# Attention and two MoE layers on one core: scores of batches 1 to 3 from float16 parts, with q and k turned by DMA

## The chip, the cores and the metric

The kernel runs on one core of one Trainium2 chip, in one launch. The metric is the device time of the launch in microseconds; lower is better. Three runs of the kernel before took 1101.78, 1102.73 and 1103.06 us, a median of 1102.73.

## What is computed

Attention with rotary position encoding (4 batches, 8 heads, 576 positions, 64 dimensions a head), then two MoE layers over 2304 tokens, all to float32 accuracy:

```
q_rot, k_rot = rotate(q), rotate(k)
scores = (q_rot @ k_rot.T) / sqrt(64)
scores = scores - max(scores, axis=-1)
attn = exp(scores); attn = attn / (sum(attn, axis=-1) + 1e-9)
x = attn @ v                                   # per batch and head, then tokens x 512
h = maximum(maximum(x @ w1, x @ w2), x @ w3)   # 512 -> 768
y = h @ w_out                                  # 768 -> 512
h2 = y @ w_in                                  # 512 -> 2048
out = (h2 * sigmoid(h2)) @ moe2_w_out          # 2048 -> 512
```

## The kernel before

**Attention.** Two heads form a pair; a batch has four pairs, so there are 16. A pair has five query tiles (four of 128 positions, one of 64), which makes 80 tiles in all. The order is: for each batch, tiles 0 and 1 of its four pairs, then tiles 2 to 4 of its four pairs; so all four pairs of a batch must be ready within the first eight of its twenty tiles. Numbered through, batch 1 begins with tile 20, batch 2 with tile 40, batch 3 with tile 60.

`attention()` issues one tile a step. `tile_scores` computes 128 rows of scores against 576 keys of both heads into the single PSUM buffer `s` (three banks): one matmul with the small block matrix `kd` for the 64 last keys of each head (L355), then three float32 matmuls that use 64 rows of the array each, the first for one head and the other two for the other (L358). `tile_max` takes the row maxima with their sign turned on VectorE (`nb`, L365), and two exponentials on ScalarE read `s` with that as their bias (L372). A step later `tile_norm` divides (L382 to L385), and two steps later `tile_turn` transposes the weights on TensorE (L401); `av` multiplies with v (L416, L420).

**Preparing a pair.** `load_qk` brings q and k of the pair into a `raw` tile (three buffers). `qk_rope` rotates them in place, for batch 0 on VectorE, later on GpSimd in nine instructions (L311 to L315). `qk_turn` turns them with nine float32 transposes on TensorE (L326, L332) and copies the result out of PSUM into `T` and `kd` with two instructions of ScalarE (L328, L333) and three of VectorE (L330, L336). `at(j, ...)` binds these calls to a step j: the rope six tiles before the pair's first tile, the turn three before.

**Beside it.** MoE 1 of a batch runs on TensorE between the tiles of the next one (`group`, L484, three float16 passes for each product of weights and values that are each split in two float16 parts); its results are evacuated by ScalarE and VectorE (L500 to L509). In the same time the weights of MoE 2 are read, narrowed on VectorE, GpSimd and ScalarE (L205, L206, L219, L220, L135) and written to scratch memory (`narrow_w2`). MoE 2 follows at the end (L484 and L728).

**What sets the order.** The program is issued step by step as above, and a list scheduler then orders each engine's instructions. On the chip each engine, and each engine's DMA queue, works its list strictly in that order. SyncE (SP) issues nearly all DMAs.

## Time and profile before

| | |
|---|---|
| median of the runs | 1102.73 us |
| the profiled execution | 1099.8 us, its span 1098.0 us |
| TensorE (PE) busy | 1019.9 us, 93% |
| VectorE (DVE) busy | 568.4 us, 52% |
| ScalarE (ACT) busy | 501.0 us, 46% |
| GpSimd (POOL) busy | 242.3 us, 22% |
| mean granted TensorE clock | 0.978 of full speed |

The span is the time from the first to the last instruction of the program. An engine's busy time counts its instructions but not its waits, register work or DMA issues. PEld is TensorE's loading of weights, which runs beside the matmuls. The matmuls overlap in the array, so the start of one to the start of the next says more than the length of one. A float32 matmul shows as two records in the trace (L355 x2 is one, L358 x6 are three). L484 is both MoE layers' helper, so its rows are told apart by time and shape.

### The profile page before, as it was taken

To read this page: it belongs to the slowest core of one execution; us is meant where nothing else is said; L and a number is where in the kernel's file an instruction comes from. 1 tells how busy PE (TensorE), PEld (TensorE's weight loads), DVE (VectorE), ACT (ScalarE), POOL (GpSimd) and SP (SyncE) were. 2 spreads that over 40 slices of the span, in tenths; PEclk is the share of its full clock that TensorE was granted. 3 is DMA by queue.
4 is the path that set the end of the run, shared out by engine and by line. 5 is a ranking of instruction groups with operands and counts; after the bars stand their busy time and mean duration, and the time that the engine had idled before them with its cause. 6 is when DMAs were issued, how large, how long until landed. Compare 5 with 4: busy or idle time off the path is not lost.

```text
span 1098.0 us, 16337 instructions
## 1 busy us (share of the span) xinstructions
PE 1019.9 (93%) x6250; PEld 625.9 (57%) x6250; DVE 568.4 (52%) x1108; ACT 501.0 (46%) x1200; POOL 242.3 (22%) x255
## 2 busy tenths in 40 slices
PE   2487899999998999999999988999999999999997
PEld 1344675766675776667766566644444444444554
DVE  5958667533577475475565568323434123423322
ACT  3668786645766667666677731122212012101111
POOL 1596117700136441051111126100000000000000
PEclk9789998999999999999999999999999999999999
DMA  7634022300334422132323173000101000100000
GB/s 195 192 109 125 13 91 57 98 1 7 98 94 126 125 87 94 44 90 91 88 87 91 63 284 120 13 13 10 49 10 48 20 20 1 39 20 1 20 20 20
DMA packets 79390, 76.10 MB, mean 69 GB/s; under 512 B 44752, under 2 KB 61648, under 8 KB 78288
## 3 DMA queue, kind: packets, MB, share of 16 engines
q1 hardware_dynamic: 75760, 65.03, 19.7%
q10 hardware_dynamic: 3552, 10.03, 2.7%
q8 instruction: 49, 0.80, 0.3%
q14 instruction: 29, 0.24, 0.1%
HBM read 57.21 MB, written 17.83 MB: 68 GB/s over the span
## 4 chain that ended last, share of the span: by engine, by line
PE 73%; DVE 5%; POOL 2%; DMA 1%; ACT 1%; issue 1%; DVEq 0%; SPq 0%; POOLq 0%
PE m L484 37%; PE o L728 17%; PE s L358 6%; PE tr L401 5%; PE xp L420 5%; PE s L355 1%; POOL wi L155 1%; PE xp L416 1%; PE tr L326 1%; DVE wi L158 1%; DVE nb L365 1%; DMA z<-in_moe_w_out_dram 1%; ACT e L372 1%; DVE vmax L145 1%; DVE wo L158 1%
## 5 line engine op out<-in xcount | busy, mean ns | idle before, releaser
L484 PE MATMUL m<-x,w 128*128 128x320 f16 (+1 forms) x1632 | 230.4, 289 | 7.5 <-ACT t L500 3.9
L728 PE MATMUL o<-wo,g 128*128 128x512 f16 x828 | 193.2, 379 | 0.0
L484 PEld LDWEIGHTS <-w 128*128 128x128 f16 x1632 | 157.1, 99 | 58.6 <-issue 18.3
L484 PE MATMUL m<-yt,wi 128*128 128x512 f16 (+1 forms) x920 | 189.8, 358 | 0.0
L714 ACT ACTIVATE gt<-m,ch 128x512 f32<-128x512 f32 (+1 forms) x80 | 51.5, 644 | 297.0 <-PE m L484 282.6
L365 DVE TENSOR_REDUCE nb<-s 128x2 f32<-128x1152 f32 (+1 forms) x80 | 108.3, 1353 | 81.8 <-PE s L358 81.5
L728 PEld LDWEIGHTS <-g 128*128 128x128 f16 x864 | 84.5, 98 | 99.7
L484 PEld LDWEIGHTS <-wi 128*128 128x128 f16 x920 | 89.6, 98 | 89.4
L372 ACT ACTIVATE e<-s,nb 128x576 f32<-128x576 f32 (+1 forms) x160 | 116.6, 734 | 48.7 <-DVE nb L365 40.1
L401 PE MATMUL tr<-ident,e 128*128 128x128 f32 (+1 forms) x720 | 113.1, 273 | 16.0 <-ACT pt L405 6.9
L385 ACT ACTIVATE e<-e,rec 128x576 f32<-128x576 f32 (+1 forms) x160 | 114.9, 766 | 15.8 <-DVE rec L383 15.7
L157 DVE TENSOR_SCALAR g<-gt,sg 128x512 f16<-128x512 f32 (+1 forms) x80 | 36.7, 458 | 162.8 <-ACT gt L714 162.8
L206 POOL TENSOR_SCALAR z<-z 128x256 uint16<-128x256 uint16 x64 | 53.6, 838 | 269.6 <-DVE z L205 255.6
L401 PEld LDWEIGHTS tr<-ident,e 128*128 128x128 f32 (+1 forms) x720 | 80.0, 142 | 41.9 <-ACT pt L405 10.8
L358 PE MATMUL s<-T 64*128 64x512 f32 (+5 forms) x480 | 103.0, 508 | 0.0
L405 ACT ACTIVATE pt<-tr 128x384 f32<-128x384 f32 (+1 forms) x160 | 70.2, 452 | 42.5 <-PE tr L401 41.7
L420 PE MATMUL xp<-pt,vd 128*64 128x256 f32 (+1 forms) x512 | 88.4, 422 | 0.0
L358 PEld LDWEIGHTS s<-T 64*128 64x128 f32 (+1 forms) x480 | 55.2, 185 | 37.4 <-issue 15.3
L484 PE MATMUL m<-h,wo 128*128 128x256 f16 (+1 forms) x512 | 73.9, 287 | 0.0
L502 DVE SCALAR_TENSOR_TENSOR t<-m,t 128x256 f32<-128x256 f32 (+1 forms) x96 | 43.4, 452 | 48.8 <-PE m L484 48.0
L420 PEld LDWEIGHTS xp<-pt,vd 128*64 128x64 f32 x512 | 38.0, 137 | 35.9 <-issue 17.3
L484 PEld LDWEIGHTS <-wo 128*128 128x128 f16 x512 | 49.2, 98 | 15.5 <-issue 3.1
(158 smaller groups left out, 1069.8 us busy)
## 6 DMA issues: line engine op xcount, KB each, us to landing
z<-in_moe_w_in_dram SPq DMA_DIRECT2D x32, 256.0 KB, 3.2
z<-in_moe_w_out_dram SPq DMA_DIRECT2D x32, 256.0 KB, 3.0
w<-in_moe_w_dram ACTq DMA_DIRECT2D x6, 768.0 KB, 6.7
wo<-in_moe_w_dram ACTq DMA_DIRECT2D x6, 768.0 KB, 4.8
qk<-in_q_dram SPq DMA_DIRECT2D x32, 128.0 KB, 3.0
qk<-in_k_dram SPq DMA_DIRECT2D x32, 128.0 KB, 3.0
vd<-in_v_dram SPq DMA_DIRECT2D x16, 256.0 KB, 2.9
zwi<-z SPq DMA_DIRECT2D x32, 128.0 KB, 2.9
```

Of the source, the lines that this page charges most:

```text
L206: nc.gpsimd.tensor_scalar(out=q[:, :, 2], in0=q[:, :, 1], scalar1=step, scalar2=off, op0=ALU.mult, op1=ALU.add)
L358: nc.tensor.matmul(s[0:n, o:o + m], qs[r], kt[r, a:a + m], start=True, stop=True)
L365: x = nc.vector.tensor_reduce(out=nb[0:n], in_=s[0:n, 0:1152].rearrange("p (h k) -> p h k", h=2), op=ALU.max, axis=AX.X, negate=True)
L372: x = nc.scalar.activation(out=e[0:n, HK[g]], in_=s[0:n, HK[g]], func=AF.Exp, bias=nb[0:n, g:g + 1], accum_out=sm[0:n, g:g + 1])
L385: nc.scalar.activation(out=e[0:n, HK[g]], in_=e[0:n, HK[g]], func=AF.Copy, scale=r[0:n, g:g + 1])
L401: nc.tensor.transpose(tr[:, i * n:(i + 1) * n], e[0:n, c * P:(c + 1) * P], ident[0:n, 0:n])
L405: nc.scalar.activation(out=to, in_=of, func=AF.Copy)
L420: nc.tensor.matmul(xp[r, 0:n], v4[:, g, c, :], pt[:, c + 5 * g, :], start=False, stop=(c == 3))
L484: nc.tensor.matmul(ps[:, 0:n], l, r, start=(i == 0), stop=(i == len(passes) - 1))
L502: nc.vector.scalar_tensor_tensor(out=t, in0=ps[:, 0:n], scalar=2.0 ** -22, in1=part[-1], op0=ALU.mult, op1=ALU.max)
L714: nc.scalar.activation(out=gt, in_=ps[:, 0:n], func=AF.Silu, scale=ch)
L728: nc.tensor.matmul(ps, l, r, start=(f == 0 and i == 0), stop=(f == NF2 - 1 and i == 2))
```

## The change

For batches 1 to 3 (12 of the 16 pairs, 60 of the 80 tiles), q and k are split after the rotation into two float16 parts each, high and low, with a power of two as scale for q and one for k. Batch 0 keeps the float32 way (`qk_turn32`, `tile_scores32`), with `kd` now a part of `T`.

- `qk_max`: three absolute maxima over the raw pair on VectorE, before the rotation. `qk_scale`: three transposes of one column and a small matmul on TensorE, a maximum and five tiny instructions on VectorE; the result is the two scales and the product of their inverses.
- `qk_turn`: ScalarE writes the high parts, six instructions (L366); VectorE subtracts them from the scaled values for the low parts, seven instructions (L367). High and low parts are stacked in `w` (now two buffers) so that one contraction over 128 rows sums high times high and low times high. The low parts of k stand in `fl`, a single tile. Three transposing DMAs on SP's queue (L387 to L389) turn 9, 9 and 6 blocks of 128 × 128 into `T`. Nothing of this uses TensorE or PSUM.
- `tile_scores`: eight float16 matmuls in place of four in float32; the last three multiply the high parts of q by the low parts of k, with 64 rows of the array each.
- `tile_max`: one more instruction on ScalarE (L474) multiplies the maxima by the inverse scale, and the exponentials take that as their scale.
- The steps: the load nine tiles before a pair's first tile, maxima eight before, rope and scale seven, turn five.

```diff
-    w_p = right("w_p", 1)
+    w_p = right("w_p", 2)
...
+    fl = [once.tile([P, 6, P], F16, name=f"fl{i}") for i in range(1)]
...
+    def qk_max(b, hp):
+        t = raw_t[b, hp]
+        m = small.tile([P, 3], F32, tag="qkm", name="qkm")
+        nc.vector.tensor_reduce(out=m[:, 1:2], in_=flat(t[:, 16:18, :]), op=ALU.max, axis=AX.X, apply_absolute_value=True)
+        x = [
+            nc.vector.tensor_reduce(
+                out=m[:, i:i + 1], in_=flat(t[:, lo:lo + 8, :]), op=ALU.max, axis=AX.X, apply_absolute_value=True
+            ) for i, lo in ((0, 0), (2, 8))
+        ]
...
+    def qk_scale(b, hp):
+        m = qkm_t.pop((b, hp))
+        ps = ps_m.tile([P, 512], F32, tag="m", name="m")
+        for i in range(3):
+            nc.tensor.transpose(ps[0:1, i * P:(i + 1) * P], m[:, i:i + 1], ident)
+        t = small.tile([1, 2], F32, tag="qkx", name="qkx")
+        nc.vector.tensor_reduce(out=t, in_=ps[0:1, 0:3 * P].rearrange("p (i x) -> p i x", i=2), op=ALU.max, axis=AX.X)
+        nc.tensor.matmul(ps[:, 384:386], ones, t, start=True, stop=True)
+        s, i = scale_of(ps[:, 384:386], 2, "qk", qks_p)
...
     def qk_turn(b, hp):
...
+        act(four(qh), head(0), s[:, 0:1])
...
+        for g in range(2):
+            act(
+                kh[:, g, 5:9, :].rearrange("p c (u d) -> p c u d", u=2),
+                t[:, 8 + g:16:2, :].unsqueeze(2).to_broadcast([P, 4, 2, D]), s[:, 1:2],
+            )
+        for g in range(2):
+            with tc.issue_after(last["max"]):
+                stt(four(ql)[:, g], head(0)[:, g], s[:, 0:1], four(qh)[:, g])
+            stt(L[:, 1:5, g * D:g * D + D], head(8)[:, g], s[:, 1:2], kh[:, g, 5:9, 0:D])
...
+        T = t_p.tile([P, 24, P], F16, tag="T", name="T")
+        nc.sync.dma_start_transpose(out=T[:, 0:9, :], in_=F[:, 0:9 * P])
+        nc.sync.dma_start_transpose(out=T[:, 9:18, :], in_=F[:, 9 * P:18 * P])
+        nc.sync.dma_start_transpose(out=T[:, 18:24, :], in_=L.rearrange("p c e -> p (c e)"))
...
     def tile_scores(key):
...
+        qa, qb = T[:, t * P:t * P + n], T[:, 1152 + t * P:1152 + t * P + n]
+        ka, kb, kl = T[:, 576:1152], T[:, 1728:2304], T[:, 2368:2944]
+        mm(0, qa, ka, 64, 512, **b0)
+        mm(512, qa, ka, 0, 64, **b0)
+        mm(512, qa, T, 3008, 64, **b1)
+        mm(576, qb, kb, 0, 448, **b0)
+        mm(1024, qb, kb, 448, 128, **b0)
+        mm(0, qa[lo], kl[lo], 64, 512, **b1)
+        mm(576, qb[hi], kl[hi], 0, 448, **b1)
+        mm(1024, qb[hi], kl[hi], 448, 128, **b1)
...
     def tile_max(key):
...
+            nc.scalar.activation(out=nb[0:n], in_=nb[0:n], func=AF.Copy, scale=inv)
...
-        at(u - 6 if i > 3 else i - 4, qk_rope, b, hp, nc.vector if i < 4 else None)
-        at(u - 3, qk_turn, b, hp)
+        if i > 3:
+            at(u - 8, qk_max, b, hp)
+            at(u - 7, qk_rope, b, hp)
+            at(u - 7, qk_scale, b, hp)
+            at(u - 5, qk_turn, b, hp)
+        else:
+            at(i - 4, qk_rope, b, hp, nc.vector)
+            at(u - 3, qk_turn32, b, hp)
```

The scheduler orders the changed program anew. Three places follow. The first is TensorE at the first tile of batch 2 (tile 40), in the kernel before: the four float32 matmuls of the scores, the transpose for the scale of v, and the transposes of a later pair (`qk`, `tr`).

```order
L484 LDWEIGHTS w_0_127
L484 MATMUL m_3336<-x_2020,w_0_127 128x256
L355 MATMUL s_3351<-kd_0_112,T_3049 128x128
L358 MATMUL s_3351<-T_3049 128x512
L358 MATMUL s_3351<-T_3049 128x384
L358 MATMUL s_3351<-T_3049 128x128
L112 MATMUL m_3394<-ident_78,vm_2_3392 1x128
L326 MATMUL tr_3297<-ident_78,qk_2509 128x128 x4
L332 MATMUL tr_3303<-ident_78,qk_2509 128x128
```

TensorE at a tile of batch 2 in the changed kernel (`T` holds the turned float16 parts, `tr` after it is the turn of the exponentials `e`):

```order
L449 MATMUL s_4316<-T_3785 128x512
L449 LDWEIGHTS T_3785
L449 MATMUL s_4316<-T_3785 128x64
L449 LDWEIGHTS T_3785
L449 MATMUL s_4316<-T_3785 128x64
L449 LDWEIGHTS T_3785
L449 MATMUL s_4316<-T_3785 128x448
L449 LDWEIGHTS T_3785
L449 MATMUL s_4316<-T_3785 128x128
L449 LDWEIGHTS T_3785
L449 MATMUL s_4316<-T_3785 128x512
L449 LDWEIGHTS T_3785
```

Four matmuls have become eight, each with its own weight load, and no transposes of `qk` stand on TensorE there any more.

The second place is VectorE between two row maxima (`nb`) shortly before batch 2, in the kernel before (`z` is the w2 narrowing, `t` and `h` are MoE 1's evacuation, `pt` the turned exponentials, `x` the attention's result):

```order
L365 TENSOR_REDUCE nb_2824<-s_2819 128x2
L219 TENSOR_SCALAR z_2781<-z_2781 128x256
L205 TENSOR_SCALAR z_2855<-z_2_2784 128x256
L407 COPY pt_2646<-tr_2845 128x3x64
L502 SCALAR_TENSOR_TENSOR t_2888<-m_2875,t_2873 128x256
L220 SCALAR_TENSOR_TENSOR z_2781<-z_1_2774,z_2781 128x256
L502 SCALAR_TENSOR_TENSOR t_2903<-m_2890,t_2888 128x256
L383 RECIPROCAL rec_2919<-rec_2919 128x2
L509 TENSOR_TENSOR h_5_2905<-t_2903,h_5_2905 128x256
L424 SCALAR_TENSOR_TENSOR x_2020<-xp_2940,vs_1696,x_2020 128x320
L365 TENSOR_REDUCE nb_2913<-s_2908 64x2
```

and behind a row maximum at that place in the changed kernel (`fl` and `w` with L367 are the subtractions for one pair, `qkx` the maximum for the scale of the next):

```order
L465 TENSOR_REDUCE nb_3250<-s_3241 128x2
L367 SCALAR_TENSOR_TENSOR w_3041<-qk_2844,qks_3059,w_3041 128x4x64 x2
L367 SCALAR_TENSOR_TENSOR fl_0_121<-qk_2844,qks_3059,w_3041 64x64 x2
L513 COPY pt_3153<-tr_3272 128x3x128
L221 TENSOR_SCALAR z_3206<-z_3206 128x256
L207 TENSOR_SCALAR z_3332<-z_2_3209 128x256
L367 SCALAR_TENSOR_TENSOR fl_0_121<-qk_2844,qks_3059,w_3041 128x4x64 x2
L222 SCALAR_TENSOR_TENSOR z_3206<-z_1_3199,z_3206 128x256
L621 TENSOR_TENSOR h_5_3129<-t_3127,h_5_3129 128x256
L614 SCALAR_TENSOR_TENSOR t_3239<-m_3226,t_3224 128x256
L326 TENSOR_REDUCE qkx_3308<-m_3304 1x2
```

Six subtractions and a maximum for the scale now stand among VectorE's other work between two row maxima.

The third place is SP's queue before batch 2 in the changed kernel (`z` loads and `zwi` stores are the w2 narrowing, `yscr` is MoE 1's result, `vd` is v):

```order
L768 DMA z_0_3082<-in_moe_w_in_dram 128x256
L749 DMA zwi_123<-z_2940 128x256
L639 DMA yscr_122<-y_2877 128x320
L387 DMA_TRANSPOSE T_3037<-w_2818 128x9x128
L388 DMA_TRANSPOSE T_3037<-w_2818 128x9x128
L389 DMA_TRANSPOSE T_3037<-fl_0_121 128x6x128
L288 DMA vd_0_120<-in_v_dram 64x64 x2
L768 DMA z_1_3199<-in_moe_w_in_dram 128x256
L749 DMA zwi_123<-z_2950 128x256
```

The three transposing DMAs of a pair stand between the narrowing's loads and stores; what follows them on SP is issued after them.

## Rows read from the trace of the kernel before

**Rows 1.** The page: the chain that ended last, by engine and by line.
```profile
PE 73%; DVE 5%; POOL 2%; DMA 1%; ACT 1%; issue 1%; DVEq 0%; SPq 0%; POOLq 0%
```
**Rows 2.** Stretches: start and end, length, busy per engine, clock, DMA share, GB/s.
```profile
40.00:60.00 20.00, 10.88 (x39) 7.14 (x39) 19.26 (x28) 13.69 (x30) 18.40 (x13) 0.65 0.43 127
...
141.50:199.90 58.40, 55.46 (x365) 37.50 (x363) 42.59 (x87) 40.89 (x102) 32.13 (x32) 0.94 0.32 87
199.90:298.30 98.40, 98.03 (x692) 67.64 (x692) 41.95 (x80) 59.34 (x148) 18.86 (x20) 1.00 0.12 36
298.30:343.80 45.50, 42.84 (x316) 30.74 (x315) 34.31 (x78) 30.45 (x84) 20.14 (x22) 1.00 0.43 118
...
452.10:496.90 44.80, 43.20 (x316) 30.69 (x314) 29.98 (x74) 28.99 (x78) 15.59 (x16) 1.00 0.27 78
496.90:630.40 133.50, 131.09 (x915) 89.80 (x912) 75.52 (x176) 93.89 (x254) 20.78 (x25) 0.99 0.27 81
...
318.60:336.70 18.10, 16.73 (x129) 11.91 (x130) 16.76 (x30) 11.15 (x32) 12.06 (x12) 1.00 0.49 132
```
**Rows 3.** The chain in order of time, 298 to 345 us: start, length, what.
```profile
319.86 2.99 DVE vmax L145 x4
...
326.79 3.12 DVE z L205 x3
...
333.51 4.22 DMA z<-in_moe_w_in_dram
```
**Rows 4.** TensorE's timeline: start, length, engine, line, operation, tiles, count.
```profile
249.55 3.42 PE L484 MATMUL m<-x,w 128*128 128x320 f16 x24
252.81 0.38 PE L355 MATMUL s<-kd,T 128*128 128x128 f32 x2
...
254.19 0.66 PE L401 MATMUL tr<-ident,e 128*128 128x128 f32 x4
```
**Rows 5.** The page: weight loads on L484, busy us and mean ns.
```profile
L484 PEld LDWEIGHTS <-w 128*128 128x128 f16 x1632 | 157.1, 99 | 58.6 <-issue 18.3
```
**Rows 6.** TensorE's timeline, transposes of q and k, what follows them.
```profile
335.49 0.66 PE L326 MATMUL tr<-ident,qk 128*128 128x128 f32 x4 [0.50 <-DVE pt L407]
...
336.09 1.47 PE L484 MATMUL m<-x,w 128*128 128x256 f16 x12
```
**Rows 7.** Groups by line and shape, 1 to 640 us: busy us, mean ns.
```profile
L330 DVE COPY T<-tr 128x512 f32<-128x512 f32 x16 | 11.0, 686 | 8.4 <-PE tr L326 8.4
L336 DVE COPY kd<-tr 64x64 f32<-64x64 f32 x32 | 7.0, 218 | 2.7 <-ACT T L333 2.4
L145 DVE TENSOR_REDUCE vmax<-vd 128x1 f32<-128x640 f32 x16 | 11.9, 809 | 0.0
L125 DVE TENSOR_SCALAR ve<-m 128x1 f32<-128x1 f32 x4 | 0.6, 146 | 0.0
L220 DVE SCALAR_TENSOR_TENSOR z<-z,z 128x256 int32<-128x256 int32 x64 | 30.8, 481 | 1.4
L328 ACT ACTIVATE T<-tr 128x512 f32<-128x512 f32 x16 | 9.4, 590 | 11.7 <-PE tr L326 11.7
L382 ACT ACTIVATE rec<-sm 128x2 f32<-128x2 f32 x64 | 13.2, 206 | 0.8 <-DMA qk<-in_k_dram 0.6
```
**Rows 8.** Line L355: what its engine waited for (us, times).
```profile
  ACT e L372: 18.7, 18
```
**Rows 9.** DMA issues: queue, operation, count, size each, median us to landing.
```profile
z<-in_moe_w_in_dram SPq DMA_DIRECT2D x32, 256.0 KB, 3.2
...
wo<-zwo SPq DMA_DIRECT2D x4, 1024.0 KB, 16.3
```
**Rows 10.** Timelines of DVE and of GpSimd: the same instruction at different times.
```profile
322.77 0.95 DVE L219 TENSOR_SCALAR z<-z 128x256 int32<-128x256 int32 x1
...
336.61 0.28 DVE L219 TENSOR_SCALAR z<-z 128x256 int32<-128x256 int32 x1
...
322.58 0.99 POOL L311 TENSOR_TENSOR w<-qk,sin_sb 128x384 f32<-128x384 f32 x1 [9.01 <-DMA qk<-in_q_dram]
```

More of the change, by code (lines that the diff above doesn't have):

```diff
@@ L99, in fused_kernel @@
     sin_sb = once.tile([P, 9, D], F32, name="sin_sb")
-    NK, NV = 4, 6
-    kd = [once.tile([P, P], F32, name=f"kd{i}") for i in range(NK)]
+    NV = 6
     vd = [once.tile([P, 5, P], F32, name=f"vd{i}") for i in range(NV)]
+    fl = [once.tile([P, 6, P], F16, name=f"fl{i}") for i in range(1)]
     yscr = dram.tile([P, KC, NT], F32, name="yscr")
@@ L258, in constants @@
         nc.gpsimd.affine_select(out=ident, in_=ident, pattern=[[-1, P]], compare_op=ALU.is_equal, fill=0.0, base=0, channel_multiplier=1)
-        for t in kd:
-            nc.gpsimd.memset(t, 0.0)
+        for t in fl:
+            nc.gpsimd.memset(t[:, 0:6:5, :], 0.0)
         for t in vd:
@@ L318, in qk_turn @@
     def qk_turn(b, hp):
+        t, W = raw_t.pop((b, hp)), w_t.pop((b, hp))
+        s, inv = sq_t[b, hp]
+        F = W.bitcast(F16)
+        L = fl[0]
+        qh = F[:, 0:38 * D].rearrange("p (g x) -> p g x", g=2)
+        ql = F[:, D:35 * D].rearrange("p (g x) -> p g x", g=2)
+        kh = F[:, 0:36 * D].rearrange("p (g c e) -> p g c e", g=2, e=P)
+        four = lambda x: x[:, :, 0:512].rearrange("p g (c e) -> p g c e", e=P)[:, :, :, 0:D]
+        head = lambda lo: t[:, lo:lo + 8, :].rearrange("p (c g) d -> p g c d", g=2)
@@ new lines, in qk_turn @@
+        rem = t[:, 16:18, :]
+        lo, hi = slice(0, 64), slice(64, 128)
+        act = lambda out, in_, sc: nc.scalar.activation(out=out, in_=in_, func=AF.Copy, scale=sc)
+        stt = lambda out, in0, sc, in1: nc.vector.scalar_tensor_tensor(
+            out=out, in0=in0, scalar=sc, in1=in1, op0=ALU.mult, op1=ALU.subtract
+        )
+        act(four(qh), head(0), s[:, 0:1])
+        act(qh[lo, :, 512:576], rem[lo], s[lo, 0:1])
+        act(qh[hi, :, 512:576], rem[hi], s[hi, 1:2])
+        act(ql[hi, :, 512:576], rem[hi], s[hi, 1:2])
@@ L320, in qk_turn @@
         t = raw_t.pop((b, hp))
-        T = t_p.tile([P, 576 + 512], F32, tag="T", name="T")
-        K = kd[(NP * b + hp) % NK]
+        w_t.pop((b, hp))
+        T = flat(t_p.tile([P, 24, P], F16, tag="T", name="T")).bitcast(F32)
+        K = T[:, 1088:1216]
+        nc.gpsimd.memset(K, 0.0)
         for i in range(2):
@@ L358, in tile_scores @@
             nc.tensor.matmul(s[0:n, o:o + m], qs[r], kt[r, a:a + m], start=True, stop=True)
+        return s
+    def tile_scores(key):
+        b, hp, t = key
+        T, inv = T_t[b, hp]
+        if inv is None:
+            s_t[key] = tile_scores32(t, T)
+            return
+        T = flat(T)
+        n = rows(t)
+        s = ps_s.tile([P, 1536], F32, tag="s", name="s")
+        lo, hi = slice(0, 64), slice(64, 128)
+        qa, qb = T[:, t * P:t * P + n], T[:, 1152 + t * P:1152 + t * P + n]
+        ka, kb, kl = T[:, 576:1152], T[:, 1728:2304], T[:, 2368:2944]
+        mm = lambda o, l, r, a, m, **kw: nc.tensor.matmul(s[0:n, o:o + m], l, r[:, a:a + m], **kw)
+        b0, b1 = dict(start=True, stop=False), dict(start=False, stop=True)
+        mm(0, qa, ka, 64, 512, **b0)
[6 more added lines that the diff above has]
+        mm(1024, qb[hi], kl[hi], 448, 128, **b1)
         s_t[key] = s
@@ L372, in tile_max @@
             x = nc.scalar.activation(
[L373 removed]
+                out=e[0:n, HK[g]], in_=s[0:n, HK[g]], func=AF.Exp, scale=inv, bias=nb[0:n, g:g + 1], accum_out=sm[0:n, g:g + 1]
             )
@@ L446, in fused_kernel @@
         if i > 2:
-            at(first[pairs[i - 1]] - (7 if hp == 3 else 9) if hp or i < 4 else first[b, hp] - 12, load_qk, b, hp)
+            at(first[pairs[i - 1]] - (7 if hp == 3 else 9) if i < 4 else u - 9, load_qk, b, hp)
         if i == 0:
             continue
-        at(u - 6 if i > 3 else i - 4, qk_rope, b, hp, nc.vector if i < 4 else None)
-        at(u - 3, qk_turn, b, hp)
+        if i > 3:
[3 more added lines that the diff above has]
+            at(u - 5, qk_turn, b, hp)
+        else:
+            at(i - 4, qk_rope, b, hp, nc.vector)
+            at(u - 3, qk_turn32, b, hp)
     for b in range(1, B):
@@ L805, in fused_kernel @@
     last["max"] = qk_rope(*pairs[0], nc.vector).ins
-    qk_turn(*pairs[0])
+    qk_turn32(*pairs[0])
     for j in sorted(e for e in events if e < 0):
```

31 lines of the change are left out of this document (23 added, 8 removed).

## The prediction

> **What bounds the kernel now.** I read the page's chain first: TensorE makes up 73% of the chain that ended last [rows 1]. MoE 2, after 740 us, runs on TensorE and isn't touched by the change; attention and MoE 1 share the time before. I cut that time at VectorE's (DVE's) row maxima, one for each of the 80 query tiles, so that the stretches in which q and k of a later batch are prepared stand alone: tiles 16 to 23, 36 to 41 and 56 to 61, which are 141.5 to 199.9, 298.3 to 343.8 and 452.1 to 496.9 us. Two of the stretches between them show TensorE busy 98 to 99.6% of the time, DVE 43 and 57% [rows 2]. In the three preparing ones TensorE drops to 94 to 96% and DVE rises to 67 to 75%. The chain inside the second one shows why: at 319.9 and again at 326.8 us it stays 3 us on DVE (four maxima of v; pieces of the w2 narrowing), and from 333.5 on 4.2 us on a load for that narrowing [rows 3]. In its worst 18.1 us DVE is busy 16.76; at the start, 40 to 60 us, 19.26 of 20 [rows 2]. So TensorE bounds most of attention, and DVE bounds the start and part of each preparation. The change takes work from the first and gives work to the second.
>
> **The change part by part, on the profiled execution's time** (1099.8 us: span 1098.0 and 1.8 around it; the median of the runs, 1102.73, is 2.9 more).
>
> *Scores, 60 of the 80 tiles.* In a dense stretch the old tile holds TensorE from 252.81 to 254.19 us, 1.38 us [rows 4]. The new one is eight float16 matmuls. Just before, 24 float16 matmuls of 320 columns take the 3.26 us from 249.55 to 252.81 [rows 4]: 136 ns each, 0.425 ns a column. So 512, 448, 128 and 64 columns take 218, 190, 54 and 27 ns, and each tile has two of every size. But a weight load is busy 99 ns [rows 5], so I let the four short ones take 100 ns each. All in a row that is 2×218 + 2×190 + 4×100 = 1.21 us. The last three use half the rows of the array each, one head in the upper and one in the lower half, like the old three on L358. If halves run side by side, one 218 goes: 1.0. With the short loads hidden too it is 0.8. I take 1.0, between the two: 0.38 × 60 = 23 us less (10 to 35).
>
> *The turn, 12 of 16 pairs.* TensorE loses nine transposes a pair. Five of them take the 0.60 us from 335.49 to 336.09 (the fifth is L332's) [rows 6]: 0.12 each, 1.1 a pair. It gains three of one column and a tiny matmul for the scale, which at 0.12 each are 0.5. Net 0.6 × 12 = 7 us less, so TensorE has 30 us less work in all.
>
> *DVE.* Per pair, removed: L330 0.69 and L336 twice 0.22, 1.1 us [rows 7]. Added: two maxima over 512 elements and one over 128 (L145 has 640 in 0.81; by share 0.65, 0.65, 0.2), 1.5; one over 384 on one partition, 0.5 by the same row; five tiny ones at 0.15 (L125), 0.75; four subtractions of 256 elements at 0.48 (L220), 1.9; three small ones at 0.22 (L336), 0.65. That is 5.3, net 4.2 us a pair and 50 us in all. In the dense stretches DVE has room for it. For the preparing stretches I priced what the new order puts between the same row maxima: about 20, 18 and 11 us of new work (the rest stands earlier or later), less 4.5 us removed in each: 15.5, 13.5 and 6.5. If DVE can be 94% busy (the mean of 16.76/18.10 and 19.26/20 [rows 2]), its room there is 54.9−42.6 = 12.3, 42.8−34.3 = 8.5 and 42.1−30.0 = 12.1 us. The first two overrun it by 3 and 5 us: 8 us longer. In those two TensorE's own saving (14 tiles × 0.38 and 8 pairs × 0.6, 10 us) then buys nothing. At the start the maxima of two pairs come between the second and fourth row maximum, where DVE is full: 3 us more.
>
> *ScalarE.* Per pair 2.4 us (three copies of 512 elements at 0.59 by L328, three small ones at 0.21 by L382) for the 0.8 removed (0.59 and 0.2). In each tile one more instruction, 0.21 us by L382 [rows 7], stands between the maximum and the exponentials, so the single score buffer comes free about 0.25 us later. L355 waited for the exponentials 18 times in 80 tiles [rows 8]; that is 14 times in 60, 3 us. Otherwise TensorE has MoE 1 work at hand, and ScalarE has room (59 of 98 us busy in the longer dense stretch [rows 2]). If that cover failed in every tile, it would be 15 us.
>
> *Transposing DMAs.* Three a pair on SP's queue (288, 288 and 192 KB), which wait there for DVE and ScalarE with the w2 loads behind them. No such DMA is in the trace. The nearest row is 256 KB landed in 3.2 us, the far one 1024 KB in 16.3 [rows 9]. So three take 10 to 49 us, one after the other; I take 11, near the closest size. The turn comes five tiles ahead (37 us, since 18 tiles take the 133.5 us from 496.9 on [rows 2]), so this is hidden, at nothing. The page "DMA: Bandwidth & Descriptors" of the Trainium skill, section "Latency and other measured facts", gives a transposing DMA 261 GB/s; by it the three would take an estimated 3 us, and no row here shows it.
>
> Sum: −30 + 8 + 10 + 3 + 3 = −6 us: 1093.8 in the profile, 1096.7 against the median shown.
>
> **The rivals.**
>
> *TensorE's saving arrives whole.* If the new work falls into DVE's gaps, the loss terms vanish: −30, 1073. For it: DVE idles 25 to 33% even of the preparing stretches [rows 2]. Against it: the chain through DVE at 320 us [rows 3].
>
> *Slower: DVE's subtractions swell beside GpSimd.* The same instruction on L219 took 0.28 us at 336.61 and 0.95 at 322.77; at the slow place GpSimd had just begun a rope, at 322.58 [rows 10]. GpSimd is busy 68 of the 148.7 us of the preparing stretches [rows 2], 46%, and a rope instruction takes 1.0 us. If each of the seven new subtractions of a pair is held for half of one, 46% of the time, that is 0.23 × 7 × 12 = 19 us of DVE, most of it where DVE then binds: about +15 on the forecast, 1112. From +6 us on the change is slower than the kernel before. The page "SBUF — State Buffer" of the Trainium skill, section "Who interferes with whom", speaks for it: a DVE instruction with two SBUF inputs contends with a GpSimd one that reads SBUF, and the later one blocks for the whole instruction. The new subtractions have two such inputs. But L220 has two as well, and its mean, such neighbours included, is 0.48 us [rows 7]; so this isn't the likeliest.
>
> *Slower: the transposes land late.* The tile that DVE writes for the third one (`fl`) is single, and the next pair's write to it comes two tiles, about 15 us, later. If the three take longer than that, DVE, which works its list in order, waits there with the row maxima behind it. At 20 us it is 5 us for each of nine pairs, 45, or 1142. In a mild form only the w2 loads behind them on SP are late, as one was already for 4.2 us [rows 3]: 12 × 1.5 = 18, 1115.
>
> *The scores don't get much shorter.* With 1.21 us a tile they give 10 instead of 23: 1110.
>
> **How the numbers follow.** Forecast 0.45 (its own range 1087 to 1104), whole saving 0.17, GpSimd 0.18, late transposes 0.12, scores 0.08. A measurement of this kernel can tell about 0.2% (2.2 us) from no change. Faster: the whole saving and three quarters of the forecast's weight, 0.51, and a little from mild forms of the others: 0.52. Same: a fifth of the forecast's and some of the slower cases': 0.13. Slower: 0.35. The time is the forecast's, 1096.7. The range from 1077 takes in the upper part of the whole saving, to 1117 the cases of GpSimd, of the scores and of mildly late transposes.
>
> **What would show it.** Right: score tiles of about 1.0 us on TensorE; DVE 44 to 54 us busier; TensorE's idle time grown in the preparing stretches and at 40 to 60 us; MoE 2 as before. For the whole saving: preparing stretches no longer than before. For GpSimd: subtractions of 256 elements above 0.6 us in the mean. For late transposes: landings above 5 us a piece, and DVE or TensorE waiting for them. I am wrong in kind if the dense stretches don't get shorter by some 0.3 us a tile.

## The result and the profile after

The changed kernel takes 1107.69 us (median of 7 runs, 1105.25 to 1111.21); the kernel before, run beside it, 1101.43 (1098.04 to 1103.06, 7 runs). The ratio is 1.0052 (95% interval 1.0039 to 1.0066): 0.5% slower, where 1096.7 and faster was forecast. The profiled execution's span (first to last instruction) is 1106.1 us, 8.1 longer than before.

Cut at the same row maxima, the two spans (and those of five experiments told below) divide like this, in us. "Preparing" is tiles 16 to 23, 36 to 41 and 56 to 61 together, "dense" the stretches between and behind them. Orders A and B are the changed kernel's work with its instructions in two other orders.

| stretch | before | after | order A | order B | DVE part alone | subtractions twice | scales of one, z moved |
|---|---|---|---|---|---|---|---|
| tiles 0 to 15 | 141.5 | 138.3 | 139.0 | 140.4 | 152.1 | 138.1 | 144.4 |
| preparing, 20 tiles | 148.7 | 178.1 | 166.0 | 169.0 | 165.1 | 176.2 | 143.8 |
| dense, 44 tiles | 340.2 | 320.9 | 324.6 | 319.3 | 358.5 | 331.1 | 327.7 |
| behind tile 79 | 467.6 | 468.8 | 468.9 | 476.0 | 467.9 | 475.1 | 467.0 |
| span | 1098.0 | 1106.1 | 1098.5 | 1104.7 | 1143.6 | 1120.5 | 1082.9 |

So TensorE's saving came, 19 us of it in the dense stretches, and the preparing stretches took 29 back. All three of them grew, by 7.5, 16.2 and 5.7 us. The windows of the changed kernel (length, then busy time and instructions of PE, PEld, DVE, ACT and POOL, granted clock, DMA share, GB/s), which answer to [rows 2]:

```profile
138.30:204.20 65.90, 54.59 (x357) 34.67 (x357) 55.86 (x133) 51.06 (x123) 35.26 (x33) 0.91 0.58 124
204.20:300.00 95.80, 92.36 (x669) 60.30 (x666) 44.49 (x86) 63.85 (x155) 16.37 (x18) 0.97 0.13 40
300.00:361.70 61.70, 48.40 (x354) 33.08 (x353) 56.44 (x127) 43.61 (x114) 34.83 (x36) 0.92 0.58 138
361.70:466.70 105.00, 102.55 (x758) 67.48 (x760) 66.91 (x163) 83.24 (x218) 24.20 (x27) 1.00 0.35 100
466.70:517.20 50.50, 42.52 (x318) 28.84 (x315) 40.57 (x96) 37.15 (x95) 23.75 (x25) 0.90 0.56 117
517.20:637.30 120.10, 116.10 (x857) 76.18 (x855) 73.04 (x169) 97.80 (x264) 20.60 (x25) 0.97 0.32 95
```

The first, third and fifth row are the preparing stretches. In them DVE is busy 80 to 91% of the time (67 to 75% before) and TensorE idles 32.6 us in all (7.2 before). TensorE's clock is 0.90 to 0.92 of 2.4 GHz there, 0.94 to 1.00 before. Of TensorE's waits in them 25.1 us end with DVE, against 5.6 before (11.3 of 20.9 us in order A, 20.9 of 25.5 in order B). The largest (who waited for whom: us in total, times, longest; the first two rows from the first stretch, then two from the second and one from the third):

```profile
PE m L327 <- DVE qkx L326: 3.1, 2, 2.3
PE tr L507 <- DVE pt L513: 3.0, 4, 1.9
PE m L596 <- DVE t L614: 4.7, 2, 3.4
PE m L117 <- DVE amax L116: 4.0, 1, 4.0
PE m L114 <- DVE t L614: 3.3, 1, 3.3
```

L327 makes the scale of q and k, L114 and L117 that of v; L614 evacuates MoE 1. Over the whole profile DVE is busy 616.6 us instead of 568.4 and ScalarE 550.9 instead of 501.0. The chain that ended last has less TensorE and twice the DVE of [rows 1]:

```profile
PE 67%; DVE 10%; POOL 3%; issue 3%; ACT 2%; DMA 2%; SPq 1%; DVEq 0%; POOLq 0%; ACTq 0%
```

A score tile on TensorE's timeline (start, length, engine, line, operation, tiles, count), against the 1.38 us of [rows 4]: seven matmuls hold it from 250.82 to 251.76, and the eighth, behind a piece of MoE 1, for 0.16 us. Over all 60 tiles L449 is busy 68.0 us by the page, 1.13 a tile.

```profile
250.82 1.00 PE L449 MATMUL s<-T 128*128 128x512 f16 x7
251.76 1.80 PE L596 MATMUL m<-x,w 128*128 128x320 f16 x12
253.49 0.23 PE L449 MATMUL s<-T 64*128 64x128 f16 x1
253.65 0.66 PE L507 MATMUL tr<-ident,e 128*128 128x128 f32 x4
```

DVE's new instructions and ScalarE's, by line and shape over 1 to 640 us (count, busy us, mean ns):

```profile
L367 DVE SCALAR_TENSOR_TENSOR fl<-qk,qks,w 128x256 f16<-128x256 f32 x24 | 12.9, 567 | 1.7 <-ACT w L366 1.5
L367 DVE SCALAR_TENSOR_TENSOR w<-qk,qks,w 128x256 f16<-128x256 f32 x24 | 12.0, 540 | 0.0
L367 DVE SCALAR_TENSOR_TENSOR fl<-qk,qks,w 64x64 f16<-64x64 f32 x24 | 7.7, 364 | 0.4
L311 DVE TENSOR_REDUCE qkm<-qk 128x1 f32<-128x512 f32 x24 | 16.0, 675 | 5.8 <-DMA qk<-in_q_dram 5.4 <-DMA qk<-in_k_dram 0.4
L128 DVE TENSOR_SCALAR qke<-qke 128x2 int32<-128x2 int32 x12 | 3.9, 324 | 0.1
L127 DVE TENSOR_SCALAR qke<-m 128x2 f32<-128x2 f32 x12 | 1.7, 145 | 1.7 <-PE m L327 1.5
L474 ACT ACTIVATE nb<-nb,qkv 128x2 f32<-128x2 f32 x48 | 14.0, 293 | 21.4 <-DVE nb L465 21.1
L478 ACT ACTIVATE e<-s,nb,qkv 128x576 f32<-128x576 f32 x96 | 78.9, 826 | 1.5 <-PE tr L507 0.3
L478 ACT ACTIVATE e<-s,nb 128x576 f32<-128x576 f32 x32 | 23.3, 736 | 6.2 <-DVE nb L465 6.2
```

The subtractions take 0.54 to 0.57 us where 0.48 was put down, the small ones 0.36 (one of three 0.48) for 0.22. And DVE's timeline inside the second preparing stretch, at a place where it has hardly a gap:

```profile
326.60 0.49 DVE L128 TENSOR_SCALAR qke<-qke 128x2 int32<-128x2 int32 x1
327.12 0.92 DVE L129 TENSOR_SCALAR qks<-qke 128x2 int32<-128x2 int32 x1
327.96 0.15 DVE L130 TENSOR_SCALAR qki<-qke 128x2 int32<-128x2 int32 x1
328.03 1.23 DVE L621 TENSOR_TENSOR h<-t,h 128x256 f16<-128x256 f32 x1
329.18 0.95 DVE L330 TENSOR_TENSOR qkv<-qki 128x1 f32<-128x1 f32 x1
330.06 1.34 DVE L465 TENSOR_REDUCE nb<-s 128x2 f32<-128x1152 f32 x1
331.32 2.98 DVE L147 TENSOR_REDUCE vmax<-vd 128x1 f32<-128x640 f32 x4
```

Operations on one or two values a partition last 0.15 or 0.9 us. GpSimd's rope instructions, which lie beside them:

```profile
325.11 2.92 POOL L343 TENSOR_TENSOR w<-qk,sin_sb 128x384 f32<-128x384 f32 x3 [2.09 <-DVE rec L489]
327.97 3.11 POOL L344 TENSOR_TENSOR qk<-qk,cos_sb 128x384 f32<-128x384 f32 x3
```

The turning DMAs land as early as taken (queue, operation, count, median us to landing), 3.3 + 3.3 + 2.8 for the 11 put down:

```profile
T<-w SPq DMA_TRANSPOSE x24, 3.3
...
T<-fl SPq DMA_TRANSPOSE x12, 2.8
```

### The profile page after: what moved, and what is told of

Read it like the earlier page. It is cut to its first block, busy times and chain, and to the rows that moved or that the text cites. A ratio compares the mean times of both kernels' runs of the same rounds, so it can differ in the third digit from the quotient of the medians.

```text
span 1106.1 us, 16556 instructions
## 1 busy us (share of the span) xinstructions
PE 999.0 (90%) x6202; PEld 595.9 (54%) x6202; DVE 616.6 (56%) x1264; ACT 550.9 (50%) x1308; POOL 239.3 (22%) x256
## 4 chain that ended last, share of the span: by engine, by line
PE 67%; DVE 10%; POOL 3%; issue 3%; ACT 2%; DMA 2%; SPq 1%; DVEq 0%; POOLq 0%; ACTq 0%
PE m L596 35%; PE o L840 17%; PE xp L526 5%; PE tr L507 4%; PE s L449 4%; DVE nb L465 2%; PE xp L522 1%; POOL wi L157 1%; DVE w L367 1%; DVE wi L160 1%; DVE z L221 1%; DVE fl L367 1%; POOL wo L157 1%; DVE pt L513 1%; DMA qk<-in_q_dram 1%
## 5 line engine op out<-in xcount | busy, mean ns | idle before, releaser
L596 PE MATMUL m<-x,w 128*128 128x320 f16 (+1 forms) x1632 | 231.5, 291 | 14.8 <-DVE t L614 7.6
L596 PEld LDWEIGHTS <-w 128*128 128x128 f16 x1632 | 158.3, 99 | 70.1 <-issue 30.2
L596 PE MATMUL m<-yt,wi 128*128 128x512 f16 (+1 forms) x920 | 189.8, 358 | 0.0
L596 PEld LDWEIGHTS <-wi 128*128 128x128 f16 x920 | 89.6, 98 | 89.4
L507 PE MATMUL tr<-ident,e 128*128 128x128 f32 (+1 forms) x720 | 115.9, 282 | 18.7 <-ACT pt L511 8.0
L478 ACT ACTIVATE e<-s,nb,qkv 128x576 f32<-128x576 f32 (+1 forms) x120 | 98.5, 825 | 1.7 <-PE tr L507 0.3
L511 ACT ACTIVATE pt<-tr 128x384 f32<-128x384 f32 (+1 forms) x160 | 69.6, 453 | 21.9 <-PE tr L507 21.5
L596 PE MATMUL m<-h,wo 128*128 128x256 f16 (+1 forms) x512 | 71.9, 288 | 1.5 <-DVE wo L160 1.3
L449 PE MATMUL s<-T 128*128 128x512 f16 (+1 forms) x480 | 68.0, 303 | 2.1 <-ACT e L478 1.9
L614 DVE SCALAR_TENSOR_TENSOR t<-m,t 128x256 f32<-128x256 f32 (+1 forms) x96 | 43.4, 452 | 43.4 <-PE m L596 35.4
L596 PEld LDWEIGHTS <-wo 128*128 128x128 f16 x512 | 49.0, 98 | 17.9 <-issue 3.2
L160 DVE SCALAR_TENSOR_TENSOR g<-gt,sg,g 128x512 f16<-128x512 f32 (+1 forms) x80 | 55.7, 696 | 2.5
```

The costliest lines, as they stand in the source:

```text
L160: nc.vector.scalar_tensor_tensor(out=l, in0=x, scalar=s, in1=h, op0=ALU.mult, op1=ALU.subtract)
L449: mm = lambda o, l, r, a, m, **kw: nc.tensor.matmul(s[0:n, o:o + m], l, r[:, a:a + m], **kw)
L478: x = nc.scalar.activation(out=e[0:n, HK[g]], in_=s[0:n, HK[g]], func=AF.Exp, scale=inv, bias=nb[0:n, g:g + 1], accum_out=sm[0:n, g:g + 1])
L507: nc.tensor.transpose(tr[:, i * n:(i + 1) * n], e[0:n, c * P:(c + 1) * P], ident[0:n, 0:n])
L511: nc.scalar.activation(out=to, in_=of, func=AF.Copy)
L596: nc.tensor.matmul(ps[:, 0:n], l, r, start=(i == 0), stop=(i == len(passes) - 1))
```

## Experiments

Each is compared with runs of the kernel before on the same chip; the changed kernel itself stands at 1.0052. Ratios below 1 are faster than the kernel before.

**DVE's work.** Theory A: DVE, full in the preparing stretches, sets their length. First, the change's DVE part alone, in the kernel before:

```diff
+            at(u - 8, more_max, b, hp)      # maxima over 512, 512 and 128
+            at(u - 7, more_scale, b, hp)    # one over 384 on one partition, five tiny
         at(u - 6 if i > 3 else i - 4, qk_rope, ...)
+            at(u - 4, more_sub, b, hp)      # four subtractions of 256, three of 64
```

> The change's DVE part alone: the kernel before with DVE instructions of the same kinds and sizes that the change adds for each of 12 pairs (two maxima over 512 elements and one over 128 eight tiles ahead, one over 384 on one partition and five tiny ones seven ahead, four subtractions of 256 elements and three of 64 four ahead), their results used by nobody. Scores, turning and ScalarE stay as they were. It is 5.3 us a pair, some 60 us of DVE, 40 of them in the preparing stretches, where TensorE was idle for 7 us. Theory A (DVE's extra work, where it is full, is the loss): 12 to 25 us slower, 1113 to 1126, with TensorE idle 15 to 30 us more there. Theory G (the loop through GpSimd's rope, ScalarE, DVE and the turning DMA): DVE's instructions fill its gaps, 1100 to 1108.

1143.36 us, ratio 1.038 (1.0345 to 1.0415): 42 us slower, more than expected. DVE's busy time rose by 80 us, not 60, to 648.7. Only 16 us of the loss lie in the preparing stretches; the start takes 11 and the dense stretches 18, which got shorter in the changed kernel. TensorE's busy time at 1.2 GHz, 35.1 us before, is 75.2. The preparing windows:

```profile
152.10:220.70 68.60, 58.82 (x357) 39.49 (x355) 57.47 (x122) 40.79 (x101) 30.13 (x28) 0.85 0.23 63
325.50:375.90 50.40, 44.59 (x310) 31.26 (x309) 44.00 (x97) 31.34 (x84) 22.19 (x22) 0.93 0.36 100
494.80:540.90 46.10, 40.91 (x291) 28.92 (x289) 38.06 (x87) 28.46 (x76) 16.62 (x16) 0.96 0.24 69
```

DVE is at 83 to 87% in them and TensorE idle 20.8 us: much of the picture of the changed kernel, without its scores. Second, the subtractions twice:

```diff
-        for g in range(2):
+        for g in (0, 1, 0, 1):
             ... stt(...)        # and the three small ones twice
```

> The changed kernel with each of the seven subtractions of a pair done twice, with the same result: 33 us more of DVE in the preparing stretches and a little outside, nothing else. Theory A: each us of DVE there costs 0.5 to 0.9, 1124 to 1137. Theory G: the turning DMA of a pair starts some 3 us later and the rope after it with it, but the turn is five tiles ahead: 1109 to 1118.

1123.38, ratio 1.0206 (1.0172 to 1.0239): 15.7 us over the changed kernel for 40 us more DVE (656.5). That is 0.6 us under theory A's range and above G's. But it didn't fall where A put it. The preparing stretches:

```profile
138.10:210.20 72.10, 55.38 (x368) 35.21 (x365) 70.23 (x159) 50.94 (x123) 39.29 (x35) 0.93 0.48 111
296.80:347.00 50.20, 41.66 (x306) 28.05 (x305) 47.93 (x110) 39.22 (x101) 25.93 (x27) 0.93 0.57 141
465.70:519.60 53.90, 40.66 (x294) 27.81 (x290) 49.77 (x113) 35.76 (x91) 25.00 (x25) 0.84 0.49 106
```

They are no longer than in the changed kernel (176.2 against 178.1; 7 to 10 longer than in orders A and B), although DVE works 15 us more in them: it is 92 to 97% busy, 95% in the mean. The loss lies in the dense stretches (10 us) and behind tile 79 (6). Third, without them:

```diff
-            stt(four(ql)[:, g], ...)   # and the other six; wz, fl zeroed once
+    wz = [once.tile([P, 19 * D], F32, name=f"wz{i}") for i in range(1)]   # stacked parts, in place of w
```

> The changed kernel without its seven DVE subtractions per pair: the low parts of q and k are zeros, written once. ScalarE's high parts, the maxima, the scales, the turning by DMA and all matmuls stay. In the changed kernel's three preparing stretches (138.3 to 204.2, 300.0 to 361.7 and 466.7 to 517.2 us, 178.1 us in all) the subtractions hold DVE for 12.2, 11.6 and 8.9 us, 32.7 in all. Theory A (DVE, full in these stretches, sets their length, and most of it is plain extra work): the stretches get 20 to 30 us shorter together and the kernel takes 1080 to 1089 us. Rival C (ScalarE's scaling holds the score buffer): the stretches keep their length within 5 us, 1103 to 1108. Rival D (the transposing DMAs make the loads behind them late): the same, 1103 to 1108.

1098.17, 0.9978 (0.9962 to 0.9995): 9.5 us gained, under a third of the DVE time: 9 us short of A's range, and outside those of C and D. Only its time is read here. It had to give the parts a tile of their own, which by itself costs (below, e7): against that run it gains 17.

**GpSimd's rope.** Rival B: DVE's instructions swell beside it. The rope of batches 1 to 3 was left out of both kernels:

```diff
-        for lo, hi in ((0, 18),) if eng else ((0, 6), (6, 12), (12, 18)):
+        for lo, hi in ((0, 18),) if eng else ():
```

> The changed kernel without the rotation (rope) that GpSimd applies to q and k of batches 1 to 3; GpSimd's other work stays. In the changed kernel, DVE's instructions in the three preparing stretches take about 30 us more than their own shortest tenth (8.1, 14.2 and 7.6), in the kernel before 15.6. Rival B (DVE's small instructions swell beside GpSimd's rope, and that is what lengthened the stretches): nearly all of these 30 us go, 1078 to 1085. Theory A (mainly plain extra work): a part of them goes, since GpSimd's rope is busy only half of the time, 1092 to 1100. Rivals C and D: 1103 to 1108.

> The control to the run before: the kernel before without the rotation of batches 1 to 3 on GpSimd. Theory A: its preparing stretches were only partly bound by DVE, so it gains little, 1093 to 1099, and the changed kernel without rope stays level with it (within 6 us either way). Rival B: it gains 5 to 10 us less than the changed kernel does by the same edit, so that the changed kernel without rope is at least 10 us faster than this one.

1085.03 (0.985, 0.9824 to 0.9875) and 1090.14 (0.9901, 0.9874 to 0.9929). The changed kernel gains 22.7 us and the one before 10.3; DVE's busy time falls by 30.7 (to 585.9) and by 18.5. The first is at the edge of B's range, but the two kernels without rope are 5 us apart, as A expected, and not 10. So the rope swells DVE's work by 12 us more in the changed kernel than in the one before. The 12 us more of time needn't all be swelling: without the rope its own time too is gone from the way of each pair, and orders spread (below). In the preparing stretches alone DVE's busy time falls from 152.9 to 127.8 us and, in the kernel before, from 107.0 to 97.6. The tiny operations show the swelling, without rope:

```profile
L128 DVE TENSOR_SCALAR qke<-qke 128x2 int32<-128x2 int32 x12 | 1.9, 157 | 0.1
L127 DVE TENSOR_SCALAR qke<-m 128x2 f32<-128x2 f32 x12 | 1.8, 147 | 2.8 <-PE m L327 2.7
```

L128 falls from 324 to 157 ns; L127, which reads PSUM, stays. The four tiny lines on SBUF together fall by 5.7 us, all subtractions by 4.0; the rest is older work, the narrowing of w2 above all.

**ScalarE's step between maximum and exponentials** (rival C). Doubled, left out (with the pointer in the exponentials), and alone in the kernel before:

```diff
+            nc.scalar.activation(out=nb2[0:n], in_=nb[0:n], func=AF.Copy, scale=inv)  # e12
-            nc.scalar.activation(out=nb[0:n], in_=nb[0:n], func=AF.Copy, scale=inv)   # e13
+            nc.scalar.activation(out=nb[0:n], in_=nb[0:n], func=AF.Copy, scale=inv)   # e14, inv = c1[0:n]
```

> The changed kernel with ScalarE's scaling of the row maxima done twice in 60 tiles (the first into a tile that nobody reads): 0.295 us more between the maximum and the exponentials of each, 18 us of ScalarE. Rival C (ScalarE's step there holds the single score buffer): 10 to 18 us slower, 1118 to 1126. Theories A and G: TensorE has other work at hand, 1107 to 1113.

> The changed kernel without ScalarE's scaling of the row maxima and without the scale pointer of the exponentials: the parts are made with a constant scale of one. The maxima and scales of q and k are still computed, and used by nobody, so DVE's and TensorE's work is the same. ScalarE loses 0.295 us a tile and 2 times 0.09 us at the exponentials, 28 us in all. Theory C (this step, in series between maximum and exponentials, holds the score buffer): as much gained as its doubling lost, 20 to 35 us, 1073 to 1088. Theory A (DVE's extra work is the loss): 1100 to 1107.

> The change's part on ScalarE between maximum and exponentials alone: the kernel before with the row maxima of batches 1 to 3 scaled by a constant one on ScalarE, and the same pointer as the scale of the exponentials. Nothing is left out. Theory C: 15 to 30 us slower, 1116 to 1131. Theory A: ScalarE has room in the kernel before, 1101 to 1107.

1138.64 (1.0345, 1.032 to 1.037), 1113.41 (1.0097, 1.0077 to 1.0118) and 1104.65 (1.0038, 1.002 to 1.0056). Doubling cost 31 us, leaving it out gained nothing and lost 6, adding it alone cost 2.8. The last two speak against C: each is far outside what it expected (e13 misses A's range too, by 6 us). Why a second 0.29 us a tile cost 31 isn't settled: 18 us of it lies in the dense stretches, where TensorE idled 9 us more and waited 5.3 us for the exponentials in the last one.

**Maxima and scales of q and k, and the step, all left out:**

```diff
-            at(u - 8, qk_max, b, hp)
-            at(u - 7, qk_scale, b, hp)
+        nc.gpsimd.memset(cs, 1.0)      # the constant scale
```

> The changed kernel with constant scales of one: the maxima of q and k, the scale that is made from them (three transposes, a matmul and seven DVE instructions a pair), ScalarE's scaling of the row maxima and the scale pointer of the exponentials are left out; the high and low parts, the turning and the matmuls stay. The maxima of q and k are about 2.75 us of DVE a pair, 33 us in all; ScalarE loses 0.295 us a tile and 2 times 0.09 us at the exponentials, 28 us in all. Theory A: the preparing stretches get 15 to 22 us shorter, the dense ones within 3 us as before, 1085 to 1093. Rival C (ScalarE): the dense stretches too get shorter, by 0.1 to 0.3 us a tile, and the whole falls to 1075 to 1083. Rival B: 1098 to 1104, since the rope still swells what is left.

1102.72 (1.0015, 0.9998 to 1.0033): 5 us gained, 10 short of A's range. The preparing stretches shrank by 21.9 us as A expected, but the start, the dense stretches and the end grew by 17.5. DVE's busy time fell by only 13.5 us of 33, partly since the subtractions swelled more (those into w from 540 to 737 ns).

**The loop through w, and late transposes** (theories G and D).

```diff
+    hl = once.tile([P, 19 * D], F32, name="hl")                    # e7: w_t[b, hp] = hl
-        nc.sync.dma_start_transpose(out=T[:, 0:9, :], ...)         # e11: all three twice
+        for _ in range(2): nc.sync.dma_start_transpose(...)
```

> The changed kernel with the stacked high and low parts in a tile of their own (hl, one buffer), and the rope's scratch w back to one buffer that only GpSimd uses. In the changed kernel GpSimd waited 8 times, 58.5 us in all, for the turning DMA to read w before it could start the next rope. Nothing is left out. Theory G: without that wait ropes come earlier, ScalarE and DVE no longer stand at a late pair's instructions, 1094 to 1102. Theory A: DVE's work is the same, 1104 to 1109. Theory F: no change by itself, 1104 to 1109.

> The changed kernel with each of a pair's three turning DMAs issued twice into the same tile: w is held 3 to 7 us longer, SP's queue holds 4 us more a pair, and the DMA engines move twice the bytes of it. Theory G (the loop through w's two buffers paces the pairs) and rival D (loads behind the turning DMAs are late): 10 to 30 us slower, 1118 to 1138. Theory A: within 4 us of the changed kernel, 1104 to 1112.

1115.10 (1.0126, 1.0094 to 1.0159) and 1119.78 (1.016, 1.013 to 1.019). GpSimd's 58.5 us of waiting for the turning DMA were gone in e7, and the kernel was 7 us slower: the ropes came earlier, into the start, which took 11.7 us longer, while the preparing stretches got 11.3 shorter. G's own prediction failed. Double turning cost 12 us: the lower end of what G and D expected, and outside A's range. Each DMA landed as early as before (3.4 and 2.8 us), and the preparing stretches got 3 us longer, the dense ones 5. So D in its mild form isn't refuted: in the changed kernel SP stood 46.5 us in all waiting for the subtractions in front of L387, with the loads behind it.

**TensorE's clock** (theory F).

```diff
+            for _ in range(5):
+                nc.tensor.matmul(s[:, 1152:1536], W1.h(1)[:, 0:P], W1.h(1)[:, 0:384], start=True, stop=True)
```

> The changed kernel with five extra float16 matmuls of 384 columns behind the scores of each of the 20 tiles 16 to 23, 36 to 41 and 56 to 61, into columns of the score buffer that nobody reads: 0.8 us a tile, 16 us of TensorE at full clock, in stretches where it was idle for 32.6 us. TensorE's records at half clock held 35.1 us of its busy time in the kernel before and 67.7 in the changed one. Theory F (the half clock after idle time is a large part of the loss): less busy time at half clock, 1098 to 1104. Theories A and G: the extra work falls partly into idle time and partly adds to the tiles, 1108 to 1122.

1106.56 (1.0049, 1.0029 to 1.0068): 16 us more of TensorE's work cost nothing. TensorE idled 97.5 us instead of 107.1, and 51.0 us of its busy time lay at 1.2 GHz instead of 67.7. The preparing stretches, which hold the added work, got 3 us longer. So TensorE's own work bounds them little. F's gain didn't come. Whether the extra work raised the clock isn't shown: other edits of the changed kernel, without such work, have 44 to 77 us at 1.2 GHz.

**The w2 narrowing (z) out of the preparing stretches**, in the changed kernel, the kernel before, and with scales of one:

```diff
-            for _ in range(1 + j % 2 if j > 31 else 0):
+            for _ in range(2 if j >= 24 and not (36 <= j <= 42 or 56 <= j <= 62) else 0):
```

> The changed kernel with the narrowing of the w2 weights (z) moved out of the three preparing stretches: its steps start at tile 24 instead of 31, two a tile, none at tiles 36 to 42 and 56 to 62. Nothing is left out. In the changed kernel's preparing stretches the narrowing holds DVE for about 1.9 us and GpSimd for 0.83 us a step, and 9 steps fall into the second and third stretch each. Theory A (DVE is full there, and relief of it shortens them): the second and third stretch lose 10 to 17 us each, the dense stretches, where DVE has room, at most 5 of it, 1085 to 1095. Theory G (the runs with one piece of DVE work taken away gave back less than a third of it, so the loop rope on GpSimd, high parts on ScalarE, low parts on DVE, turning DMA, and back to the rope's buffer paces the pairs): the narrowing isn't in that loop, 1100 to 1106. Theory F (a lower granted clock after TensorE's idle time is what costs): idle time goes with the narrowing, 1092 to 1100.

> The control: the same move of the w2 narrowing in the kernel before. Its preparing stretches have 7 us of TensorE idle time in all, so all theories expect little: 1094 to 1102. If the move gains as much here as in the changed kernel, its gain there says nothing about the change.

> Constant scales of one (as in the fourth run) and the w2 narrowing moved out of the preparing stretches (as in the fifth), together. Left out: the maxima and scales of q and k. DVE loses some 13 us in sum and 20 more in the preparing stretches. Theory A: with DVE no longer full there, 1085 to 1094. If something else fills the time that is freed, as in the fifth run, 1098 to 1104.

> As the run before it, and the MoE 1 work that is handed out per tile is 10000 columns in the preparing tiles and 7200 in the others, instead of 8000 everywhere (68 tiles: 5% less in attention, the rest after it). Theory A: TensorE's idle time in the preparing stretches (24 us with scales of one) is filled with work that the dense stretches lose, 1080 to 1092. If DVE or ScalarE is the limit there even so, the preparing stretches get longer by the added work, 8 to 15 us, and the dense ones shorter by as much: within 4 us of the run before it.

1106.98 (1.0063, 1.0041 to 1.0084), 1096.43 (0.9962, 0.9944 to 0.9981), 1085.04 (0.9846, 0.9825 to 0.9867) and 1089.53 (0.9883, 0.9864 to 0.9902). Alone the move missed A's range by 12 us: it shortened the preparing stretches by 14 us, in which DVE was then 78% busy, and gave it all back (105 more matmuls were put into the last dense stretch). With scales of one it brings what A expected:

```profile
144.40:205.60 61.20, 52.06 (x327) 31.77 (x326) 49.17 (x98) 47.79 (x115) 44.56 (x42) 0.86 0.61 137
301.50:345.60 44.10, 40.74 (x320) 28.34 (x319) 31.79 (x66) 32.35 (x78) 27.77 (x27) 1.00 0.51 109
449.50:488.00 38.50, 35.67 (x283) 24.77 (x280) 27.46 (x58) 29.65 (x73) 18.39 (x18) 1.00 0.48 87
```

DVE is busy 108.4 us in the preparing stretches instead of 152.9, at 71 to 80%, and they are shorter than in the kernel before (143.8 against 148.7). This version beats both kernels, by 1.5% the one before (1.2% when both have z moved), on these inputs; what it gives up is the scaling that would keep q and k of any size within float16. Redistributed MoE 1 work (e16) added 4 us.

**Order alone.** Every edit above also changed the order in which the planner puts DVE's instructions. These two change little else (372 and 278 of DVE's 1207 rows stand elsewhere):

```diff
+    at(13, lambda: nc.vector.memset(junk_p.tile([P, 768], ...), 0.0))    # e18: at(22, ...)
```

> The changed kernel with one DVE memset of 768 bfloat16 values (under 1 us) at tile 13, whose only effect is that the planner puts the instructions behind it in another order (372 of DVE's 1207 rows). If order alone matters by several us: anywhere from 1098 to 1118, away from the changed kernel's 1107.7 by more than 2.5. If the extra work explains the result by itself: 1106 to 1110.

> The same memset at tile 22, which gives another order (278 of DVE's 1207 rows elsewhere). The same expectation: 1098 to 1118 if order matters, 1106 to 1110 if it doesn't. The spread of the two and of the changed kernel is how far a difference between two of the edited kernels may come from order alone.

1098.51 (0.9971, 0.9955 to 0.9987) and 1104.08 (1.0026, 1.0007 to 1.0046): one order of the same work is faster than the kernel before. The kernel before was not run in other orders. The preparing windows of the first:

```profile
139.00:200.30 61.30, 54.25 (x381) 34.92 (x378) 55.00 (x125) 49.55 (x123) 33.75 (x32) 0.97 0.53 126
296.30:350.90 54.60, 47.09 (x338) 32.27 (x335) 47.50 (x111) 40.89 (x109) 31.93 (x33) 0.91 0.66 159
460.70:510.80 50.10, 43.77 (x324) 29.53 (x321) 40.99 (x98) 37.26 (x95) 24.00 (x25) 0.90 0.54 115
```

DVE's share is again 82 to 90%. Orders of the same work spread over 9 us, so no difference below that between two edited kernels is put down to its edit here; e1's, e4's, e5's, e7's, e8's and e13's against the changed kernel are within or near it. Three orders are few, so e10's 15.7 and e11's 12.1 are weak evidence too. The preparing stretches alone spread over 12 us.

## Why the prediction was wrong

**TensorE's saving: right.** Predicted 30 us. At 1.2 GHz a matmul takes twice its time (those of L596 with 320 columns start 136 ns apart at full clock and 267 at half, by the median), so I take half of the busy time at that level off: 1019.9 − 35.1/2 = 1002 before; 965 in the changed kernel and in both other orders. Five profiles of kernels with the old scores give 994 to 1002, so it is 29 to 37 (edits of the changed kernel that leave TensorE's work alone give 964 to 978). The score tile takes 1.1 us for 1.0 put down. The dense stretches, 20 us by the prediction's prices (44 tiles, and the turns of five pairs that lie there), lost 19, 16 and 21 in the three orders.

**DVE's total: right, with luck.** 48.2 us more busy, 50 predicted. The prices were too low: count times mean of the new lines is 82 us, 6.8 a pair for 5.3. What made up for it is that neighbouring records overlap (L129 above ends at 328.04, the next starts at 327.96), by 14 us more in all than before, and that other lines got shorter.

**The step that failed: "The first two overrun it by 3 and 5 us: 8 us longer."** The preparing stretches got 29 us longer, 17 and 20 in the other two orders; the third, which was to have room, grew too. That DVE's added work makes them longer was right. Two sizes were off. The first is the work: DVE's rose by 45.9 us there (107.0 to 152.9), not by 35.5. Swelling beside the rope is enough to explain that, since without rope it rises by 30.2 (97.6 to 127.8). The second is the room: DVE was taken to be 94% busy before a stretch grows, from its busiest 18 and 20 us. The stretches grew with DVE at 85, 91 and 80%, 86% of the whole (86 and 87% in the other orders, 85% in e9). At 94% the 152.9 us would have taken 163, at 86% they take 178, against 148.7: of the 29 us about half is the work and half the share.

These 86% aren't a limit of DVE, which reached 95% with its subtractions doubled. Before it was full the engines already waited for each other: in these stretches TensorE waited 25 us for DVE, and DVE 12 us for TensorE, 8 for ScalarE and 4 for DMAs. How much of that the order could take away is open.

That DVE's part is what costs is shown twice: alone it made the kernel before 42 us slower, with its preparing stretches 16 longer, and with it cut to 108 us in these stretches TensorE's saving came through (e15, which also lacks ScalarE's step; leaving out that step alone gained nothing). Against it stands e10, where more of it made these stretches no longer than in the changed kernel (orders alone spread them over 12 us).

The prediction's 10 us of saving that "buys nothing" was counted too high: of its 14 tiles ten have the new scores, and five turns lie in the two stretches, not eight, so by its prices it is 7.

**The rival of GpSimd** named the swelling, 19 us of DVE in the new subtractions and 15 of time. Measured are 4 us in the subtractions, 12 more of DVE in all than in the kernel before, and some 12 of time, not all of it shown to be swelling: the large subtractions average 0.54 to 0.57, under its 0.6 (0.47 and 0.55 without rope), and it is the tiny operations on SBUF that double. Reductions don't swell (L311 675 ns with rope and 680 without). The Trainium skill, page "SBUF — State Buffer", section "Who interferes with whom", says so too: `tensor_scalar` can enter a mode that takes the port pair shared with GpSimd, a reduction on trn2 never does; L128 and L311 agree.

**Smaller terms.** The start got 3 us shorter, not longer. ScalarE got 50 us busier where its prices give 32; the 3 us put down for it can't be told from the spread of orders (e13, e14). Late transposes: they land in 3 us as taken, and that rival is refuted for landing; its mild form, loads that are late behind them on SP, is open (e11). The sum left out TensorE's clock: the busy time at 1.2 GHz rose from 35.1 to 67.7 us, 19 us of the rise in the preparing stretches and 10 in the start. Two windows of the second preparing stretch show it fall: TensorE is busy for 6.70 of 10.10 us at full clock, and then at half.

```profile
343.00:353.10 10.10, 6.70 (x57) 4.93 (x56) 9.63 (x21) 9.66 (x25) 6.67 (x7) 1.00 0.75 174
353.10:360.00 6.90, 4.46 (x21) 2.90 (x22) 6.57 (x18) 2.02 (x10) 5.29 (x6) 0.51 0.56 137
```

Half of that rise, 16 us, is lost to the clock, and 29 us more idle time stand beside 37 saved: that is the 8 us. How much of the 16 lies on the path is open.

**The sign.** The three orders take 1098.5, 1104.1 and 1107.7. Against the one order of the kernel before that was run, the change is worth −3 to +6 us; that it came out slower is the order that it happened to get. The failed step is off in all three; with order A the sign would have been right by luck. A forecast of −6 with a verdict on the sign is finer than the spread of the orders.
